# A decode step of two attention and two gated layers on one core: TensorE multiplies a constant in its pauses

## The chip, the cores and the metric

The kernel runs on one core of one Trainium2 chip. What counts is the device time of one execution in microseconds. A core has a matrix engine (TensorE, PE in the profile, with PEld for its weight loads), a vector engine (VectorE, DVE), an engine for activation functions and copies (ScalarE, ACT), a general engine (GpSimd, POOL) and SyncE (SP), which here does nothing but issue the loads from HBM. Sixteen DMA engines move what is issued. SBUF is the memory on the core that matmuls read, PSUM (eight banks of 128 x 512 numbers in f32) the one they write.

## The reference

Four sequences decode one token each. The same attention layer and the same gated layer are applied twice:

```
x = A_x                                    # 4 x 1 x 512
x = x + attention(layernorm(x))            # 32 q heads, 8 kv heads, head size 128
x = x + gated(layernorm(x))
x = x + attention(layernorm(x))            # same weights, same caches
x = x + gated(layernorm(x))

attention(x): q = x @ wq                   # 512 x 4096
              k, v = last 2048 rows of the caches (4 x 8 x 8192 x 128)
              softmax(q k^T / sqrt(128)) v, then @ wo      # 4096 x 512
gated(x):     (sigmoid(x @ w_gate) * (x @ w_up)) @ w_down  # 512 x 1792, 1792 x 512
```

All of it is bf16 in memory. The K and V that are read are 16.8 MB each; 69.4 MB are read from HBM in all, since most of V, wq and the gated layer's weights are read once per layer.

## The kernel before, in words

**Plan, order and semaphores.** The program first makes a list of operations (`P.op`): engine, name, an estimated duration, what it reads and writes by token, and which PSUM banks it touches. `_schedule` orders each engine's list by estimated start times; only TensorE's operations that are written after the first gated layer (`P.chain = True`) keep the order in which they are written. The loads on SyncE always keep theirs. `_assign_sync` then gives every operation one semaphore that its last instruction raises, and the waits that its readers need. Two operations of TensorE need no wait between them. An operation that touches a bank waits for another engine's operations on that bank.

**Memory.** SBUF has 50 slots of 128 x 2048 bf16. The 16 K tiles (1 MB, one for each kv head and pair of sequences) take 32 slots and stay for both attentions. V tiles, wo, wq and the gated weights go through what is left. A load into a place that was used before waits until its last reader has raised its semaphore. In the first gated layer the places form a ring: gate loads go where V lay, up loads go where gate, wq or V lay, down loads go where gate and up lay, the second wq's loads where up and down lay.

**The first attention** (`attn_first`) goes over the kv heads 0 to 7. For head h: VectorE transposes the K tiles in place (line 927, four pieces of 128 x 1024); TensorE writes a mask into a bank (line 945) and adds the scores (line 956, 16 matmuls of 512 columns, four column strips of the array side by side); VectorE takes the maximum (line 969 and after); ScalarE takes the exponential (line 984); TensorE turns the probabilities with the constant matrix `perm` (line 997); ScalarE copies them (line 999) and VectorE transposes them (line 1004). Then TensorE multiplies by V (line 1047: 32 matmuls of 8 columns for each of a head's two V tiles), scales and permutes (lines 1056, 1066, 1071) and multiplies by wo into the bank WB (line 1238). Head h + 2 is begun before head h is ended.

**The first gated layer** (`glu`) begins with the layer norm: a sum (line 794), a matmul with 1/512 (line 799), differences, a second matmul for the variance (line 820). Gate and up take four loads each; every load brings four matmuls of 448 columns on four column strips (line 1426), written to bank WB. VectorE transposes each result (line 1435). w_down comes in four loads with 12 or 16 matmuls of 4 columns each (line 1496), added in bank CB; line 1513 adds the sum to x.

**The second q and the second attention.** A layer norm again, then 32 matmuls with wq (line 868) as eight parts, of which the last loads arrive during the layer. The second attention (`attn_second`) goes over the heads 7 to 0 with K as it lies in SBUF: mask and scores on the same lines, V with 512-column matmuls (line 1130), VectorE's transposes behind them (line 1140). The second gated layer ends with w_down on line 1471 and the store.

The diff touches `layer_norm`, `softmax_unit`, `pv_unit`, `wo_unit` and `glu`.

## Time and profile before

| | |
|---|---|
| runs | 176.71, 176.71, 177.76 us (median 176.71) |
| profiled execution | 177.47 us, span 175.8 us |
| TensorE busy | 107.3 us, 1663 matmuls |
| VectorE busy | 105.6 us |
| ScalarE, GpSimd busy | 34.0, 23.3 us |
| loads | 69.38 MB, 96.5% of sixteen engines' span |
| mean granted clock, as recorded | 0.947 |
| chain that ended last | DMA 38%, VectorE 31%, TensorE 23% |

The page cuts the span into 40 slices of 4.4 us and gives the busy share of each in tenths; PEclk is the recorded clock of TensorE in tenths of full speed. The other views answer from the same execution: the timeline of one engine (start and duration in us, engine, line, what is written and read, how many), sums over windows (for each engine busy time and number of instructions, then clock, share of the DMA engines, GB/s), the chain that ended last (start, duration, what), and the list of loads with the time from issue to landing. A matmul's duration there holds its own latency, so sixteen in a row take less than sixteen times their mean. Landing times of single loads, their sixteen parts (one for each DMA engine) and the clock's records are read from the same trace.

### The profile page before, as it was taken

The page shows a single profiled execution, that of the slowest core. Times are in us where ns is not written, and L with a number is a line of the kernel's source. Part 1 is how long each engine was busy: PE and PEld are TensorE (multiplying, and loading weights), DVE is VectorE, ACT ScalarE, POOL GpSimd, SP SyncE. Part 2 cuts the span into 40 slices and gives each one's busy share as a digit, 9 for nine tenths or more (in the row PEclk, how much of TensorE's full clock was granted, in tenths as well). Part 3 has the DMA queues.
Part 4 walks back from the last instruction along what each step waited for, and adds up shares of the span by engine and source line. Part 5 has one row for each costly group of instructions (what it writes and reads, how often), then busy time and mean ns, then how long its engine had stood idle before and what let it go on. Part 6 is the DMA issues. An engine that isn't in the chain of part 4 may idle for free.

```text
span 175.8 us, 3937 instructions
## 1 busy us (share of the span) xinstructions
PE 107.3 (61%) x1663; PEld 55.3 (31%) x1663; DVE 105.6 (60%) x260; ACT 34.0 (19%) x89; POOL 23.3 (13%) x94
## 2 busy tenths in 40 slices
PE   0536246268566272661765566558975999877692
PEld 0203112023334151340444452143321344345531
DVE  6307997994957748377323831316496699944343
ACT  2002021322303003020030010102132354541011
POOL 6100010101101001010010000002011334534000
PEclk9999999999999999999999999999996599997558
DMA  5999999999999999999999999999999999999970
GB/s 187 423 429 429 420 421 423 406 423 423 427 412 411 422 421 420 425 406 426 423 406 425 406 399 405 403 401 390 403 394 408 425 425 416 420 420 418 419 282 5
DMA packets 12370, 69.64 MB, mean 396 GB/s; under 512 B 1336, under 2 KB 1472, under 8 KB 6336
## 3 DMA queue, kind: packets, MB, share of 16 engines
q1 hardware_dynamic: 12344, 69.38, 96.5%
q8 instruction: 13, 0.21, 0.5%
q14 instruction: 5, 0.04, 0.1%
q10 hardware_dynamic: 8, 0.00, 0.0%
HBM read 69.37 MB, written 0.00 MB: 395 GB/s over the span
## 4 chain that ended last, share of the span: by engine, by line
DMA 38%; DVE 31%; PE 23%; issue 3%; ACT 2%; SPq 1%; POOL 1%; POOLq 0%; DVEq 0%
DMA arena<-in_A_v_cache_dram 20%; DVE arena L927 10%; PE ps L956 8%; DMA arena<-in_A_wq_dram 6%; DMA arena<-in_B_w_gate_dram 5%; DVE small L969 4%; DMA side<-in_A_wq_dram 4%; DMA arena<-in_B_w_up_dram 3%; PE ps L945 3%; PE ps L1130 2%; DVE arena L1140 2%; DVE small L973 2%; DVE side L1004 2%; PE ps L1047 2%; PE ps L1426 2%
## 5 line engine op out<-in xcount | busy, mean ns | idle before, releaser
L927 DVE STREAM_TRANSPOSE arena<-arena 128x1024 f32<-128x1024 f32 x32 | 37.0, 1204 | 0.1
L1047 PE MATMUL ps<-side,arena 128*128 128x8 bf16 x576 | 18.1, 168 | 13.2 <-DMA arena<-in_A_v_cache_dram 13.1
L956 PE MATMUL ps<-arena,side 128*32 128x512 bf16 x256 | 25.8, 539 | 0.1
L1047 PEld LDWEIGHTS ps<-side,arena 128*128 128x128 bf16 x576 | 16.7, 104 | 19.6 <-DMA arena<-in_A_v_cache_dram 17.7
L969 DVE TENSOR_REDUCE small<-ps 128x1 f32<-128x512 f32 x16 | 10.9, 678 | 17.5 <-PE ps L956 17.4
L984 ACT ACTIVATE side<-ps,small 128x512 bf16<-128x512 f32 x16 | 11.0, 687 | 35.4 <-PE ps L1066 18.3
L945 PE MATMUL ps<-small,msk_s 128*32 128x512 bf16 x64 | 8.6, 530 | 14.7 <-DVE arena L927 14.1
L920 ACT CAST side<-ps 128x256 bf16<-128x256 f32 x16 | 5.9, 371 | 34.2 <-PE ps L956 25.9
L999 ACT CAST side<-ps 128x512 bf16<-128x512 f32 x16 | 9.4, 585 | 14.0 <-PE ps L997 14.0
L1013 POOL CAST small<-small 128x1 bf16<-128x1 f32 x9 | 1.7, 187 | 76.1 <-ACT side L984 76.1
L956 PEld LDWEIGHTS ps<-arena,side 128*32 128x32 bf16 x256 | 8.3, 121 | 10.7 <-issue 7.9
L997 PE MATMUL ps<-side,perm 128*128 128x512 bf16 x16 | 8.1, 507 | 4.7 <-ACT side L984 4.7
L1130 PE MATMUL ps<-arena,side 128*32 128x512 bf16 x112 | 8.5, 431 | 1.4 <-ACT side L984 1.4
L868 PE MATMUL ps<-arena,xn 128*4 128x512 bf16 x60 | 7.3, 577 | 3.2 <-DMA arena<-in_A_wq_dram 2.9
L1426 PE MATMUL ps<-arena,xn 128*4 128x448 bf16 x60 | 6.9, 537 | 3.2 <-DMA arena<-in_B_w_up_dram 1.5
L1056 DVE TENSOR_TENSOR onb<-ps,rinv 128x16 bf16<-128x16 f32 x9 | 1.7, 185 | 10.9 <-PE ps L1047 10.8
L1004 DVE STREAM_TRANSPOSE side<-side 128x256 f32<-128x256 f32 x16 | 6.9, 433 | 2.0 <-ACT side L999 1.8
L915 PE MATMUL ps<-side,eyew 32*128 32x64 bf16 x64 | 5.7, 220 | 3.3 <-ACT side L920 2.4
L945 PEld LDWEIGHTS ps<-small,msk_s 128*32 128x32 bf16 x64 | 1.7, 98 | 17.9 <-DVE arena L927 16.2
L1435 DVE STREAM_TRANSPOSE side<-ps 128x448 f32<-128x448 f32 x4 | 2.5, 634 | 7.3 <-PE ps L1426 7.3
L1140 DVE STREAM_TRANSPOSE arena<-ps 128x512 f32<-128x512 f32 x7 | 4.9, 700 | 2.6 <-PE ps L1130 2.6
L915 PEld LDWEIGHTS ps<-side,eyew 32*128 32x128 bf16 x64 | 3.4, 108 | 8.8 <-ACT side L920 5.4
(133 smaller groups left out, 136.5 us busy)
## 6 DMA issues: line engine op xcount, KB each, us to landing
arena<-in_A_v_cache_dram SPq DMA_DIRECT2D x26, 1024.0 KB, 14.8
arena<-in_A_k_cache_dram SPq DMA_DIRECT2D x16, 1024.0 KB, 24.9
arena<-in_A_wq_dram SPq DMA_DIRECT2D x4, 1024.0 KB, 7.9
arena<-in_A_wo_dram SPq DMA_DIRECT2D x3, 1024.0 KB, 26.7
arena<-in_A_v_cache_dram SPq DMA_DIRECT2D x5, 512.0 KB, 7.0
arena<-in_A_wq_dram SPq DMA_DIRECT2D x5, 512.0 KB, 7.0
arena<-in_B_w_up_dram SPq DMA_DIRECT2D x4, 448.0 KB, 6.0
arena<-in_B_w_gate_dram SPq DMA_DIRECT2D x2, 896.0 KB, 17.0
```

Source lines behind the costliest of these rows:

```text
L915: last = pe.matmul(dst[:, :, a * REP:(a + 1) * REP], eyew[32 * hh:32 * hh + 32, 96 - 32 * a:224 - 32 * a], src, start=True, stop=True)
L927: P.op("vector", "T%d_%d" % (h, t), c_dve(1024), lambda v, v32=v32: v.transpose(v32, v32), r=[("slot", 4 * h + t)], w=[("slot", 4 * h + t)])
L945: last = pe.matmul(ps[32 * gi:32 * gi + 32, bank, :], msk_s[:, :], msk_m[:, :].unsqueeze(1).broadcast_to([128, 256, 2]), start=True, stop= ...
L956: last = pe.matmul(ps[32 * gi:32 * gi + 32, bank, :], qbd[:, q0:q0 + 32], kt[:, cp // 2, cp % 2, jh * NJ:(jh + 1) * NJ, :], start=False, s ...
L969: lambda v: v.tensor_reduce(nmax[:, k2:k2 + 1], ps[:, bank, :], AXX, ALU.max),
L984: lambda a: a.activation(prow[:, :].rearrange("p (m x t) -> p m x t", x=32, t=2), ps[:, bank, :].rearrange("p (m t x) -> p m x t", x=32, t ...
L999: P.op("scalar", "pc" + tag, c_act(512), lambda a: a.copy(prow[:, :], ps[:, pb, :]), r=[("ppb", pb)], w=[("prow",)], banks=(pb,))
L1004: P.op("vector", "pt" + tag, c_dve(256), lambda v: v.transpose(et, prow[:, :].bitcast(F32)), r=[("prow",)], w=[("e", k2)])
L1047: last = pe.matmul(ps[:, ob, bp * 8:bp * 8 + 8], slot_ap(ss[j // NJ])[:, j % NJ * 128:(j % NJ + 1) * 128], ev[:, j % 2, j % 16 // 2, x0:x0 ...
L1130: last = pe.matmul(ps[32 * g:32 * g + 32, ob, :], ew[:, g, mq, t], src.rearrange("p (m t d) -> p t m d", t=2, d=128)[:, t], start=(n == 0) ...
L1140: P.op("vector", "tv" + tag, c_dve(512), lambda v: v.transpose(tv, ps[:, ob, :]), r=[("pso", k2, 0), ("pso", k2, 1)], w=[("tv", k2)], bank ...
L1426: last = pe.matmul(ps[32 * g:32 * g + NB, gub[n], 0:NF], xn[:, c * NB:(c + 1) * NB], src[:, g * NF:(g + 1) * NF], start=(c == 0), stop=(c ...
```

## The change

A new function `keep_warm` issues n matmuls with `perm` as weights and `perm` (repeated where more than 128 columns are asked for) as the moving operand, into PSUM columns that nobody reads, or reads only after a matmul that starts anew. `keep_op` makes an operation of them that follows the TensorE operation written last. They are put:

- ahead of and behind the scores of kv head 7 in the first attention (12 and 4 of 448 columns);
- behind seven of the V tiles, from the second of head 4 on (4 each, 3 behind the last), and between the two halves of the last wo (3);
- around the first gated layer's first norm (12 of 32 columns, 2 of 512), behind five of its eight gate and up parts (11 of 64), behind gate and behind up (16 of 32 each), ahead of w_down (2 of 512), behind each of its parts (2, 2, 2, 1 of 512), and behind the second q's first norm matmul (1 of 512).

Inside an operation the constants stand behind the matmul that raises the semaphore.

```diff
+        def keep_warm(pe, n, bank, c0, w):
+            last = None
+            for _ in range(n):
+                dst = ps[:, bank, c0:c0 + w]
+                src = perm[:, 0:min(w, 128)]
+                if w > 128:
+                    dst = dst.rearrange("p (a x) -> p a x", x=64)
+                    src = perm[:, 0:64].unsqueeze(1).broadcast_to([128, w // 64, 64])
+                last = pe.matmul(dst, perm[:, :], src, start=False, stop=False, skip_group_check=True)
+            return last
+
+        def keep_op(name, n, bank, c0, w, after=()):
+            return P.op("tensor", name, n * (w / 2.4 + 10.0), lambda pe: keep_warm(pe, n, bank, c0, w),
+                        w=[("cb",)] if bank == CB else [], banks=(bank,),
+                        after=tuple([o for o in P.ops if o.eng == "tensor"][-1:]) + tuple(after))
+
+        WFREE = REP * NX
+        WARM_V = {"0.%d_1" % (HKV - 4): 4, "0.%d_0" % (HKV - 3): 4, "0.%d_1" % (HKV - 3): 4, "0.%d_0" % (HKV - 2): 4,
+                  "0.%d_1" % (HKV - 2): 4, "0.%d_0" % (HKV - 1): 4, "0.%d_1" % (HKV - 1): 3}
...
+            if tag == "G0":
+                keep_op("kwL", 12, CB, SAVED_P, 32)
             P.op("tensor", "ln_sum" + tag, tm["pe_f32"],
...
+            if tag == "G0":
+                keep_op("kwG", 2, WB, 0, 512)
+            if tag == "Q":
+                keep_op("kwQ", 1, WB, 0, 512)
...
+            if tag == "0.%d" % (HKV - 1):
+                keep_op("kwS", 12, WB, WFREE, 512 - WFREE, named("pp0.%d" % (HKV - 2)))
             P.op("tensor", "S" + tag, (16 if wait else 20) * tm["pe_row"], e_s,
...
+            if tag == "0.%d" % (HKV - 1):
+                keep_op("kwT", 4, WB, WFREE, 512 - WFREE)
...
+                    keep_warm(pe, WARM_V.get("%s_%d" % (tag, bp), 0), WB, WFREE, 512 - WFREE)
                     return last
                 P.op("tensor", "PV%s_%d_%d" % (tag, h, bp), 2 * NJ * tm["pe_pair"], e_pv,
-                     r=[("slot", x) for x in ss] + [("e", k2)], w=[("pso", k2, bp)], banks=(ob,))
+                     r=[("slot", x) for x in ss] + [("e", k2)], w=[("pso", k2, bp)],
+                     banks=(ob, WB) if "%s_%d" % (tag, bp) in WARM_V else (ob,))
...
+                    if half < REP and r0 == 0:
+                        keep_warm(pe, 3, WB, WFREE, 512 - WFREE)
...
+                        if k == 0 and (c or n) and c < NC - 1:
+                            keep_warm(pe, 11, WB, NF, 512 - NF)
...
+                if k == 0:
+                    keep_op("kw%d" % n, 16, CB, SAVED_P, 32)
...
+            keep_op("kw2", 2, WB, 0, 512)
...
+                    keep_warm(pe, 2 if b < NFC else 1, WB, 0, 512)
                     return last
```

More of the change, by code (lines that the diff above doesn't have):

```diff
@@ L1499, in e_d @@
                                              start=(fc == 0 and c == 0), stop=(fc == NFC - 1), skip_group_check=True)
+                    keep_warm(pe, 2 if b < NFC else 1, WB, 0, 512)
                     return last
                 P.op("tensor", "gd%d_%d" % (k, a), (b - a) * NC * tm["pe_pair"], e_d,
-                     r=stok(s, (b - a) * D) + [("hT",)] + hts, w=[("cb",)], banks=(CB,))
+                     r=stok(s, (b - a) * D) + [("hT",)] + hts, w=[("cb",)], banks=(CB, WB))
                 done(name)
```

## The prediction

> **What bounds the kernel now.** I read the times first. The profiled execution took 177.47 us, 1.7 us more than its span of 175.8, and lies inside the runs shown (176.71 to 177.76, median 176.71). One per cent, 1.8 us, is about what a measurement of this kernel can tell from no change. My sum is made against 177.47, and its result is then set beside the median.

> The page's slices come next.

> ```profile
> PEclk9999999999999999999999999999996599997558
> DMA  5999999999999999999999999999999999999970
> ```

> The DMA engines are full from the second slice to the 38th, so 69 MB of loads are a stream without a hole. PEclk seems to say that TensorE had its full clock until slice 30. The timeline of TensorE denies it: the same scores (line 956, 16 matmuls of 512 columns) at two times.

> ```profile
> 83.05 1.93 PE L956 MATMUL ps<-arena,side 128*32 128x512 bf16 x16
> ...
> 144.61 1.08 PE L956 MATMUL ps<-arena,side 128*32 128x512 bf16 x16
> ```

> At 83 us TensorE ran at half speed; the first clock record of the trace begins at 126.41, and before it the row shows a default. TensorE is slow from the start to 126.4. The chain that ended last says where this matters.

> ```profile
> 115.67 6.58 DMA side<-in_A_wq_dram
> 122.29 0.60 PE ps L868 x4
> ...
> 124.20 1.86 PE ps L956 x14
> ...
> 133.97 1.90 PE ps L1130 x16
> ...
> 172.39 0.98 PE ps L1471 x56
> ```

> Up to 122.25 the chain is mostly loads: TensorE's work there is beside the stream. From 122.29 it holds compute alone, on a slow TensorE until 126.4 and again from 133.23 to 140.06. But the stream is only just ahead of it, as the issue list and the windows at the end show.

> ```profile
> arena<-in_B_w_down_dram SPq DMA_DIRECT2D x1, 256.0 KB, 21.9
> ...
> 169.00:170.00 1.00, 1.00 (x14) 0.62 (x14) 0.65 (x1) 0.21 (x2) 0.00 (x0) 0.50 0.81 318
> 170.00:171.00 1.00, 1.00 (x20) 0.44 (x16) 0.45 (x3) 0.52 (x3) 0.00 (x0) 0.61 0.26 100
> ```

> The last load, the end of w_down, was issued at 149.83 and landed 21.9 us later, at 171.71. TensorE starts w_down at 172.39, **0.68 us after the last landing**. (Last columns of the windows: granted clock, DMA share, GB/s.)

> **What moves the clock.** The records change only on a grid of 3.41 us: slow to fast at 126.41, back at 133.23, fast at 140.06, slow at 160.54, fast at 170.78. So I looked at windows cut on that grid.

> ```profile
> 129.82:133.23 3.41, 1.83 (x26) 0.81 (x26) 3.14 (x11) 0.47 (x3) 0.94 (x4) 1.00 1.02 399
> 153.71:157.13 3.42, 2.57 (x31) 1.79 (x31) 2.24 (x7) 1.38 (x4) 0.94 (x4) 1.00 1.00 413
> 157.13:160.54 3.41, 2.80 (x65) 1.78 (x66) 1.58 (x5) 1.42 (x4) 1.67 (x7) 1.00 1.02 422
> ```

> The third is busier than the second (2.80 against 2.57 us) and yet the clock falls after it. It is full of 8-column matmuls, so I count streamed columns, not busy time. 16 matmuls of 512 columns on four column strips take 0.89 us fast (line 1130 at 154.24), so 512 columns are 0.22 us fast, 0.43 slow. In column time at the fast rate, as a share of a window: 0.35 and 0.36 (first and third) dropped the clock, 0.40 (second) and 0.47 kept it; from slow, 0.37 and 0.38 did not raise it, 0.44 and 0.46 did. **The line lies near 0.39 of a window, either way.** The start of the grid I take as free in each execution.

> [...]

> **The change, part by part.** It adds 157 matmuls of a constant (46 of 448 columns, 44 of 32, 55 of 64, 12 of 512) with a weight load each; nothing is removed, and the order on VectorE, ScalarE, GpSimd and the DMA queue stays. They total 31,680 columns, 13.7 us fast or 27 us slow by the 512-column price, all between 78.7 and 120 us, where TensorE has pauses. Semaphores are still raised by the last real matmul, so only what is next on TensorE waits.

> 1. *Last K tiles.* TensorE idles from 78.73 to 82.65, for the transposes. 12 constants (448 columns: 0.38 us slow, 0.19 fast) fill 78.7 to 82.6-83.2; with the scores and 4 more behind, TensorE is dense for 6 to 8 us, so a whole grid window is full and the clock rises between 81.4 and 84.8. The scores may start 0.5 us late and run 1 us shorter. Cover: the V tile after next lands at 86.80. Cost nothing.

> 2. *V tiles.* One lands every 2.49 us (1 MB); 4 constants stand behind each of six, 3 behind the last. Two tiles need 8 x 448 constant columns and about 1,400 of real work, 2.1 us of 4.97: 0.42 on average, but a 3.41 us window that catches only one group holds 0.75 + 0.45 = 1.2 us, 0.35. So it will often fall. When slow, two tiles take 8 x 0.38 + 2 x 0.87 (line 1047) + about 1.2 for the rest = 6.0 us against 4.97: TensorE lags by 1 us per pair, some 2.5 us at the last V tile, and then holds only 0.31 to 0.33, so it does not recover there. The constants between the halves of the output weights and ahead of the mean add up to 2.3 us slow, 1.1 us fast, partly in pauses: first gate matmul up to 0.3 us late if fast, 3.5 us if slow.

> Who waits: the loads of w_up, w_down and wq go to places that these matmuls free. w_up's third load was issued at 106.72 and the load ahead of it landed at 111.28, a lead of 4.6 us; 1.1 us are left at 3.5 us late. At the start of the kernel the first packet moved 1.04 us after its issue. So the stream just holds, and this costs between 0 and 1 us (fewer than nothing is excluded: no load is issued earlier where the engines are full). I take 0.

> 3. *Gate, up, down.* Gate and up: 11 x 64 constants and the four real matmuls are 0.48 us per 1.12 us of load, 0.43; the clock comes back there. Slow they fill 0.45 + 0.59 = 1.04 of 1.12 us, so a lag stays but does not grow. Down: two of 512 per 1.25 us, 0.36 alone, about 0.42 from 113.5 to 119.7 with the constants around it. All of it is covered by the wq load that lands at 122.25 (the sixteen q matmuls ahead of it end at 121.6 today), unless rival C holds.

> 4. *From 122.29.* If the clock is fast: line 868 twice 0.60 to 0.39, line 945 0.62 to 0.40, line 915 0.39 to 0.28, line 956 1.90 to 1.08: **1.5 us** earlier at 126.1. Behind it VectorE carries the chain to 133; then TensorE waits for the softmax, as before, and the window there (0.35) may drop again; if it does not, 133.97 to 140.7 loses another 2.6 us (line 1130 0.86 and 0.4, 997 0.2, 945 0.2, 956 0.84, small ones 0.2). From 140 to 152 VectorE is full and nothing is gained.

> 5. *More instructions.* The 13 fetches of 16 KB on the instruction queue belong to TensorE's 3,326 instructions, so 314 more are 1.2 fetches. One at 30.44 made one of the sixteen parts of a load land 1.06 us late from there on. Cost 0 to 1.1 us, if it hits the slowest engine; taken as 0.

> **The sum.** The compute chain gains 1.5 to 4.1 us, but only 0.68 until w_down's last load is late next. After the landing at 171.71 its 8 matmuls need 0.3 us: the last matmul ends at 172.0 in place of 173.37. 177.47 - 1.4 = **176.1 us**, 0.3% under the median: no change that can be told.

> **Rivals.**
> - *B, it doesn't do what it says.* The window before 122.3 holds kwQ (0.22), sixteen q matmuls (0.87) and little else, 1.1 to 1.2 us, 0.33 to 0.35: if a grid edge falls just before 122.3, the second attention starts slow as now. Going through where the edge can lie, this is about one case in three, and in some of them part 4's second half makes up for it. Time as before, 176.7 to 177.6: 177.0.
> - *C, slower.* The constants themselves become the queue ahead of the second q. If the clock is slow from the last up load (landed 113.49) on, 4.7 us of constants, 5.3 us of real work and 1.5 us of waits stand ahead of the matmuls that need the last of the first wq loads: 125.0. Some 1.3 us of the constants lie inside those waits, which leaves 123.7, 1.4 us behind 122.29; the second attention then starts late and as slow as now: 177.47 + 1.4 = 178.9, more if part 2's lag is still there. It decides where the window that ends near 113.5 is under 0.39. Against it: the gate stage's own 0.43.
> - *D, faster.* The last landing is not fixed. The sixteen engines end between 169.2 and 171.3; the windows after 169 hold 0.81 + 0.26 + 0.03 = 1.1 us of full work, so evenly shared they would end at 170.1, 1.2 us sooner. If fetches fall otherwise, and compute gains over 2 us, 176.1 - 1.2 = 174.9, or a little less.

> **How the numbers follow.** Forecast 0.48 (175.3 to 176.7), B 0.20, C 0.17, D 0.15. D is taken as faster by over 1% (under 174.94), C as slower (over 178.48), the others as the same: 0.15, 0.68, 0.17. The range 174.8 to 177.9 leaves out C and little of D.

> **What would show it.** Right: line 956 near 1.08 us at its first use in the second attention; the first q matmul there still released by the wq load; the w_down matmuls of the end waiting for a load; line 1047's tiles after 92 us starting late behind slow constants. Wrong: the last landing well before 171, or w_down still waiting for VectorE; a DMA share below 0.9 between 105 and 122 us (the stream starved); or a first q matmul that starts long after its load.

## The result, and the profile after

The changed kernel takes **177.76 us** (median of 22 runs, 176.09 to 179.71); the kernel before, run beside it, 176.62 (22 runs, 176.04 to 177.76). The ratio is 1.0058 with a 95% interval of 1.0037 to 1.0080: slower by 0.6%, where I had forecast 0.3% faster, that is, nothing. (The ratio leaves out three runs of the changed kernel, 178.74 to 179.71 us, that fell into a slower state.) I had taken one per cent as the least that can be told from no change; with 22 runs of each kernel, 0.6% can. The profiled execution took 178.39 us, span 176.6.

The page of the kernel after, TensorE's recorded clock, the DMA engines and what they moved, in 40 slices:

```profile
PEclk9999999999999999999978978997597899995555
DMA  5999999999999999999999999999999999999970
GB/s 185 427 427 423 427 423 421 406 419 425 421 419 415 415 419 429 419 404 429 412 415 424 403 403 388 393 412 395 412 319 395 423 423 423 416 418 423 417 305 4
```

The clock moves a good deal earlier than before: its records show full speed from 83.67 to 90.49, 93.91 to 104.15, 107.56 to 121.21 and 128.04 to 134.87 us. (Ahead of 83.67 there is no record and the row shows nines again, though twelve constants of 448 columns take 4.68 us there, 0.39 each.) But it falls at 121.21, just ahead of the second attention, and the stream has a thin slice (319 GB/s, at 128 to 132 us).

TensorE's timeline at that place (start, duration, line, tiles, number; in brackets the idle time before and what ended it):

```profile
120.72 0.39 PE L894 MATMUL ps<-arena,xn 128*4 128x512 bf16 x4 [0.71 <-DMA arena<-in_A_wq_dram]
121.82 0.60 PE L894 MATMUL ps<-arena,xn 128*4 128x512 bf16 x4 [0.71 <-DMA arena<-in_A_wq_dram]
...
123.11 0.60 PE L894 MATMUL ps<-side,xn 128*4 128x512 bf16 x4 [0.16 <-DMA side<-in_A_wq_dram]
...
124.95 1.90 PE L982 MATMUL ps<-arena,side 128*32 128x512 bf16 x16
```

The constants are not in the way here: TensorE stands idle for 0.71 us twice, **waiting for loads of wq**. The load that opened the second attention at 122.29 before opens it at 123.11, and the first scores take 1.90 us, as slow as before.

The chain that ended last, from there on:

```profile
115.45 7.61 DMA side<-in_A_wq_dram
123.11 0.60 PE ps L894 x4
...
125.01 1.86 PE ps L982 x9
...
134.77 1.85 PE ps L1163 x16
...
144.06 0.61 DVE arena L1173
...
154.16 0.89 PE ps L1163 x16
...
162.93 0.87 PE ps L1078 x32
...
172.55 1.69 PE ps L1510 x56
```

The wq load was issued 0.22 us earlier than before (115.45 against 115.67) and yet ended 0.8 us later: 7.61 us in place of 6.58. Against the profile of before the chain seems to make this up by 154 us and to lose 0.7 us in the last line alone (1.69 against 0.98 us, a matter of the clock). That comparison misleads: executions of the kernel before differ among themselves by up to 1.7 us. A second profile of it, of a faster execution (176.78 us), happens to have the clock of after from 128 us on (fast from 128.14 to 134.96, slow to 138.38, fast again). Its chain, at the same steps:

```profile
122.15 0.53 PE ps L868 x4
...
124.00 1.86 PE ps L956 x12
...
133.77 1.05 PE ps L1130 x16
...
142.69 0.64 DVE arena L1140
...
152.80 0.89 PE ps L1130 x16
...
161.37 0.87 PE ps L1047 x32
...
170.98 1.69 PE ps L1471 x56
```

Step by step the kernel after is behind by 0.96, 1.01, 1.00, 1.37, 1.36, 1.56 and 1.57 us, and its execution by 1.61. **The loss begins at the one wq load**: 0.96 of the 1.57 us are there, and go down a chain of compute to the end. The 0.37 us added near 134 us are the clock: at 134.77 the kernel after starts 16 matmuls just as its fast stretch ends (134.87) and needs 1.85 us; the other starts them 1.00 us earlier and needs 1.05. Another 0.20 us come between 154 and 163 us; what adds them is not shown.

Why is that load late? A load comes in sixteen parts and counts as landed with the last (before, the last part comes at 122.25 us and the matmul that waits for it starts at 122.29). From the trace, when the parts of this load came (us; the ninth and the last four of sixteen), and the fetches of TensorE's instructions near it:

```
               9th part      last four parts                   fetches of 16 KB started at
before            121.46     121.68  121.73  121.76  122.25    103.00  119.03
before, 2nd       121.58     121.74  121.75  121.78  121.84    103.14  118.42
after             121.40     121.56  121.57  121.63  123.06    100.25  108.96  118.50
```

Fifteen parts of after are in by 121.63, earlier than before; one is at 123.06. It is late from the load on that was in flight when the fetch of 118.50 ran: the load ahead by two has fifteen parts by 119.12 and one at 120.68, the load before that none behind. The DMA view of both kernels, cut to the first 122 us, counts the fetches (queue, packets, MB, share of sixteen engines); before, then after:

```profile
q8 instruction: 8, 0.13, 0.4%
```

```profile
q8 instruction: 9, 0.15, 0.5%
```

### The profile page after: what moved, and what is told of

It is laid out like the page before. It is cut to its first block, busy times and chain, and to the rows that moved or that the text cites. A ratio compares the mean times of both kernels' runs of the same rounds, so it can differ in the third digit from the quotient of the medians.

```text
span 176.6 us, 4239 instructions
## 1 busy us (share of the span) xinstructions
PE 116.9 (66%) x1808; PEld 62.4 (35%) x1820; DVE 105.7 (60%) x260; ACT 34.1 (19%) x89; POOL 23.3 (13%) x94
## 2 busy tenths in 40 slices
DMA  5999999999999999999999999999999999999970
## 4 chain that ended last, share of the span: by engine, by line
DMA 55%; PE 18%; DVE 15%; SPq 6%; issue 2%; ACT 1%; POOL 1%; POOLq 0%; DVEq 0%
DMA arena<-in_A_v_cache_dram 48%; SPq L401 6%; DMA side<-in_A_wq_dram 4%; PE ps L1078 3%; DMA arena<-in_B_w_up_dram 3%; PE ps L791 2%; DVE small L1000 2%; PE ps L1163 2%; DVE arena L1173 2%; PE ps L982 2%; PE ps L1461 2%; DVE arena L1178 1%; DVE arena L596 1%; DVE side L1035 1%; PE ps L1271 1%
## 5 line engine op out<-in xcount | busy, mean ns | idle before, releaser
L982 PE MATMUL ps<-arena,side 128*32 128x512 bf16 x256 | 24.8, 520 | 0.0
L791 PE MATMUL ps<-perm 128*128 128x64 bf16 (+3 forms) x157 | 22.4, 283 | 0.5 <-issue 0.3
L791 PEld LDWEIGHTS ps<-perm 128*128 128x128 bf16 x157 | 8.9, 105 | 7.1 <-issue 5.6
L1163 PE MATMUL ps<-arena,side 128*32 128x512 bf16 x112 | 8.3, 422 | 1.4 <-ACT side L1015 1.4
L1461 PE MATMUL ps<-arena,xn 128*4 128x448 bf16 x60 | 5.8, 474 | 1.3 <-DMA arena<-in_B_w_up_dram 0.7
```

Of the source, the lines that this page charges most:

```text
L791: last = pe.matmul(dst, perm[:, :], src, start=False, stop=False, skip_group_check=True)
L982: last = pe.matmul(ps[32 * gi:32 * gi + 32, bank, :], qbd[:, q0:q0 + 32], kt[:, cp // 2, cp % 2, jh * NJ:(jh + 1) * NJ, :], start=False, s ...
L1163: last = pe.matmul(ps[32 * g:32 * g + 32, ob, :], ew[:, g, mq, t], src.rearrange("p (m t d) -> p t m d", t=2, d=128)[:, t], start=(n == 0) ...
L1461: last = pe.matmul(ps[32 * g:32 * g + NB, gub[n], 0:NF], xn[:, c * NB:(c + 1) * NB], src[:, g * NF:(g + 1) * NF], start=(c == 0), stop=(c ...
```

## The experiments

All ratios are to the kernel before, run on the same chip beside it (medians 176.59 to 176.72). The last columns are of the one profiled execution; between the two of the kernel before, the landing of the wq load differs by 0.41 us. Where a row shows 8 fetches, the ninth starts after that load has landed.

| | ratio, 95% interval | fetches ahead of 122 us | 9th starts | last wq part (before: 122.25, 121.84) |
|---|---|---|---|---|
| after | 1.0058 (1.0037 to 1.0080) | 9 | 118.5 | 123.06 |
| e1_tiny | 1.0087 (1.0054 to 1.0121) | 9 | 118.7 | 123.11 |
| e2_first | 1.0004 (0.9977 to 1.0031) | 8 | 126.8 | 122.61 |
| e3_second | 1.0055 (1.0025 to 1.0084) | 9 | 119.3 | 122.92 |
| e4_second_r | 1.0019 (0.9990 to 1.0047) | 9 | 119.4 | 122.98 |
| e5_shift128 | 1.0063 (1.0038 to 1.0089) | 9 | 118.6 | 123.18 |
| e6_shift64 | 1.0007 (0.9989 to 1.0024) | 8 | 125.9 | 121.98 |
| e7_after64 | 1.0090 (1.0057 to 1.0123) | 10 | 112.5 | 123.44 |
| e8_down_r | 1.0165 (1.0131 to 1.0198) | 8 | 125.8 | 121.79 |
| e9_few_r | 0.9999 (0.9966 to 1.0033) | 8 | 122.9 | 122.28 |
| e10_few | 1.0016 (0.9981 to 1.0051) | 8 | 123.2 | 122.43 |
| e11_shift256 | 1.0095 (1.0059 to 1.0131) | 10 | 103.3 | 123.62 |

### e1_tiny: the same instructions with almost no column time

```diff
         def keep_warm(pe, n, bank, c0, w):
             last = None
             for _ in range(n):
+                w = 8
                 dst = ps[:, bank, c0:c0 + w]
```

> All 157 constants stay where they are, but each streams 8 columns in place of 32 to 512: the same instructions, almost no time on TensorE (157 x 0.03 us, 4.4 us spread over 40) and no help for the clock. Three theories for the 1.1 us by which the changed kernel is slower. LATE: slow constants hold TensorE, loads that wait for its semaphores are issued late, the DMA engines run dry; then this kernel is like the kernel before, within 0.3 us. FETCH: the 314 instructions are fetched by the same DMA engines and make the slowest of them slower; then it is slower by 0.5 to 1.1 us, like the changed one. CLOCK: what counts is only how the second attention starts; it starts slow here as before, 0 us.

Ratio 1.0087. The loads of w_up are issued on time (106.69 against 106.72), the clock is slow until 127.86 (126.41 and 128.14 in the kernel before), and the wq load still ends at 123.11. So what the constants take of TensorE's time is not needed for the loss, and their number is enough; LATE falls.

### e2_first and e3_second: half of the constants each

```diff
 # e2_first: these and w_down's are left out
-                keep_op("kwL", 12, CB, SAVED_P, 32)
-                keep_op("kwG", 2, WB, 0, 512)
-                keep_op("kwQ", 1, WB, 0, 512)
-                            keep_warm(pe, 11, WB, NF, 512 - NF)
-                    keep_op("kw%d" % n, 16, CB, SAVED_P, 32)
```

```diff
 # e3_second
-        WARM_V = {"0.%d_1" % (HKV - 4): 4, ...
+        WARM_V = {}
-                keep_op("kwS", 12, WB, WFREE, 512 - WFREE, named("pp0.%d" % (HKV - 2)))
-                keep_op("kwT", 4, WB, WFREE, 512 - WFREE)
-                        keep_warm(pe, 3, WB, WFREE, 512 - WFREE)
```

> Only the constants up to the last wo: 12 + 4 around the scores of head 7, 27 behind V tiles, 3 between the halves of wo. Nothing in the gated layer, so the clock is slow again by 122 us. LATE: the first gate matmul is late by the 3 constants of wo and what TensorE still lags, 0.2 to 0.8 us in the profile, and the time rises by 0.2 to 0.6 us. FETCH: 92 instructions, a third of a fetch: 0 to 0.4 us. CLOCK: 0 us, the second attention starts as before.

> Only the constants from the gated layer's first norm on (111 of 157); the clock is slow when they begin. LATE: 12 of 32 and 2 of 512 columns ahead of the first gate matmul cost up to 0.9 us there, gate and up then keep pace: 0.4 to 1.0 us slower. FETCH: 222 instructions, 0.9 of a fetch: 0.3 to 0.8 us. CLOCK: where the window before 122 us is full enough, the first scores of the second attention take 1.1 us in place of 1.9 and the time falls by up to 1 us; where it is not, 0 us.

The 46 wide constants up to the last V tiles and wo cost nothing that can be told (1.0004). The 111 from the first norm on cost all of it (1.0055). With them the ninth fetch starts at 119.26 and the wq load ends at 122.92; without them it starts at 126.8.

The one trace of e2 does not look like its median. The execution took 177.66 us, one of the longer of twelve (176.09 to 178.12, median 176.64), and in it the first scores of the second attention start at 124.66, as in e3. There the *eighth* fetch, at 109.26, is followed by one part of w_up's third load that lands 0.88 us behind the other fifteen; the loads of w_down end 0.7 to 0.8 us later than in the kernel before, and the second q starts at 120.48 in place of 119.72. So a fetch that is not the ninth can do it too; how often it does in the executions that were not traced, no run shows.

### e4_second_r: e3, and the clock held up to the second attention

```diff
+                if k == 1 and i == 1 and c in (1, 2):
+                    keep_op("kwR%d" % c, 20, CB, SAVED_P, 32)
```

(behind the second and third part of the second q)

> As the run with the gated layer's constants alone, and 20 more of 32 columns behind the second and the third part of the second q, where TensorE waits 0.7 us each for the next wq load. They lift the window before 122 us from 0.32 of its column time by 0.08 to 0.16, over the line at 0.39. CLOCK: the first scores of the second attention take 1.1 us in the profile, the V loads that wait for them are issued 1 us or more earlier, and the time is 0.5 to 1.5 us under that of the run without these 40. LATE and FETCH: no gain from them, 0 to 0.3 us more than that run.

The clock stays up from 108.5 to 156.3. TensorE's timeline of e4 at the start of the second attention:

```profile
123.03 0.39 PE L893 MATMUL ps<-side,xn 128*4 128x512 bf16 x4 [0.59 <-DMA side<-in_A_wq_dram]
...
124.56 1.09 PE L983 MATMUL ps<-arena,side 128*32 128x512 bf16 x16
```

It starts as late as in after (the fetch is there, at 119.4), but the scores end at 125.65 in place of 126.03 before. The ratio comes back to 1.0019: much of what e3 loses seems to be won back by the fast clock (the intervals of the two overlap).

### e5_shift128 and e6_shift64: the kernel before with early instructions, and nothing else

```diff
+        def shift(n):
+            def e(pe):
+                last = None
+                for _ in range(n):
+                    last = pe.matmul(ps[:, WB, 0:8], perm[:, :], perm[:, 0:8], start=False, stop=False, skip_group_check=True)
+                return last
+            P.op("tensor", "shift", n * 50.0, e, r=perms, w=[], banks=(WB,),
+                 after=tuple([o for o in P.ops if o.eng == "tensor"][-1:]))
...
+            if tag in ("0.1", "0.2", "0.3", "0.4"):
+                shift([32, 32, 32, 32][int(tag[2]) - 1])     # e6: 16 each
```

> The kernel before with 128 multiplications of 8 columns (read by nobody) behind four early score steps of the first attention, between about 20 and 60 us, where TensorE waits for K tiles anyway. They are 256 instructions, so every fetch of TensorE's instructions moves forward by about one: in the kernel before, the 7th and 8th of the profiled fetches start at 103.0 and 119.0 us and the 9th at 132.2; here the 9th should start near 117 us, as the 9th did in the kernel after (118.5) and in the version with 8 columns everywhere (118.7). Nothing is added between 80 us and the end. FETCH (which DMA engine a 16 KB fetch delays goes by the number of the fetch, and the 9th hits the one that is last): the last load of the second q lands at 122.9 to 123.1 instead of 122.25, the second attention starts 0.7 to 0.9 us later, 177.3 to 178.3 us, ratio 1.004 to 1.009. PLACE (the loss comes from instructions that stand between 105 and 122 us, by some way other than the fetches): landing at 122.25, 176.4 to 176.9, ratio 0.998 to 1.002.

> As the one before, with 64 such multiplications in place of 128. By the order of the instructions the 8th fetch should start near 112 us and the 9th near 125, so none lies at 117 to 120 us. FETCH: if the fetch of 112 us meets a DMA engine that is ahead of the others, the last load of the second q lands at 121.8 to 122.3 and the time is 176.0 to 176.8 (ratio 0.996 to 1.001); if it meets the one that is last, the landing is at about 122.9 and the ratio 1.003 to 1.007, and the trace must show that one part alone is late by about 1 us from 112 us on. PLACE: as before, 176.4 to 176.9, landing at 122.25.

This is the test on which the cause rests. In e5 nothing of the change is there, and nothing is added behind 60 us. (The columns written are, other than the expectation says, columns of the output projection's sums, so the output differs; e11's expectation says it for all of these.) The chain of e5, and the same step of e6:

```profile
115.60 7.58 DMA side<-in_A_wq_dram
123.22 0.60 PE ps L877 x4
...
122.28 0.53 PE ps L877 x3
```

In e5 the load is issued 0.07 us earlier than before and lands 0.93 later, ratio 1.0063: as the change itself. With half as many (e6) the eighth fetch starts at 107.0 (expected: near 112) and the ninth at 125.9, the load ends at 121.98 and the ratio is 1.0007. The two intervals do not overlap. (In the traced execution of e6 the clock is up from 123.41, in that of e5 from 128.37, so their later steps are not compared.) Instructions that stand near 105 to 122 us (PLACE) are not needed for the loss.

The parts of the loads in e5 show why it is the *ninth* fetch. Sixteen parts in order, us from their median, of a load behind the 1st, 4th, 8th and 9th fetch:

```
1st   -0.2 -0.1 -0.1 -0.1 -0.1 -0.1 -0.0 -0.0  0.0  0.0  0.1  0.1  0.1  0.1  0.2  1.5
4th   -0.2 -0.2 -0.2 -0.2 -0.1 -0.1 -0.0 -0.0  0.0  0.1  0.1  0.8  1.4  1.4  1.4  1.5
8th   -1.3 -1.3 -1.2 -1.1 -1.0 -0.9 -0.6 -0.2  0.2  0.3  0.3  0.3  0.4  0.4  0.4  0.5
9th   -1.3 -1.3 -1.2 -1.1 -1.0 -0.9 -0.6 -0.2  0.2  0.3  0.4  0.4  0.4  0.4  0.5  1.9
```

With the first eight fetches the number of late parts grows, one fetch, one more part by 0.8 to 1.5 us, until about half of them are late together. The end of a load is set with the first of them and hardly moves with the next seven. The ninth meets a part that is late already, and the end of every load behind it moves by 1.4 us at once. In after, e1, e3, e4, e5, e7 and e11, where the ninth comes ahead of the last wq load, the last part falls back by 0.8 to 1.3 us against the mean of the sixteen with it; with the second to eighth it does so by 0.3 us at the most; in e6 the ninth does the same (1.2 us) behind that load. The count is not the whole of it: in e2, e9 and e10 the eighth fetch (109.26, 114.25 and 114.44) already moves the end of the loads, by 0.9, 0.5 and 0.75 us, and the ninth adds 0.4 to 1.0. Why, no run shows. That a part is one DMA engine's share fits the packets of before: between 8 and 28 us each of the sixteen parts of a load of 1 MB is eight packets of 8 KB and one of 4 bytes, and just ahead of the first twelve fetches 16.2 to 16.6 of the loads' packets are in flight on the average, during them 14.9 to 15.6. But the trace does not name engines, and no run shows whether the ninth fetch goes to the engine of the first.

### e7_after64: the change, with its fetches moved

> The kernel after, with the 64 early multiplications of 8 columns. Its fetches should start near 104, 115 and 119 us instead of 100, 109 and 118.5. FETCH: one fetch more falls between the start of w_up's loads and the second q's last landing; which engines the two meet decides, so the landing of that load is 122.2 if neither meets the last one (then 176.4 to 177.0, ratio 0.998 to 1.002), 123.1 if one does (177.4 to 178.2, ratio 1.004 to 1.009), and the time goes with the landing either way. PLACE: as the kernel after, 177.4 to 178.2, wherever the fetches fall and whenever that load lands.

Ratio 1.0090, above that of after (the intervals overlap). The ninth fetch, at 112.54, meets the last load of w_up: fifteen parts by 113.55, the last at 114.89, 1.4 us behind the load's end in the kernel before. TensorE waits for it (1.66 us), the window of the clock there holds 0.23 of column time, the clock falls, and w_down's constants run at half speed (1.03 us for two of 512; 0.59 to 0.60 in after). So the wq loads are issued late as well (115.67 before, 117.42 here), and the second q starts at 122.67 in place of 119.72. FETCH foretold a late landing (123.1; it was 123.44) but not this: once the clock is lost, the constants are the queue, and the matmuls that need that load start at 125.00, 1.6 us behind its landing. PLACE's 177.4 to 178.2 does not fit either. (This is read from one execution, of 179.41 us; the twelve spread from 176.66 to 181.28.)

### e8_down_r: only w_down's constants, and those behind the second q

```diff
+            keep_op("kw2", 2, WB, 0, 512)
+                    keep_warm(pe, 2 if b < NFC else 1, WB, 0, 512)
+                keep_op("kwQ", 1, WB, 0, 512)
+                    keep_op("kwR%d" % c, 20, CB, SAVED_P, 32)
```

> The kernel before with a constant of 512 columns at the second q's norm, 20 of 32 columns behind each of the second and third part of the second q, and the change's constants from w_down's tiles on; nothing of the change ahead of 117 us. The instructions ahead of 119 us are those of the kernel before but for a few, so its 8th fetch should stay at 118 to 119.5 us and the last load of the second q should land at 122.2 to 122.4. FETCH with CLOCK: the landing is on time and the window of the clock that ends near 122 us holds about 0.48 of column time instead of 0.33, so the second attention starts at 122.3 with its scores at about 1.1 us instead of 1.9: 175.2 to 176.2 us, ratio 0.991 to 0.997, the fastest of all. PLACE: the 40 small ones behind the second q stand in the place that costs, so 176.5 to 177.3, ratio 0.999 to 1.004.

I expected the fastest and got the slowest, 1.0165. The load was on time (121.79), as FETCH said, but the clock was not. Four rows of TensorE's timeline in e8, and below them the start of the second q in the kernel before:

```profile
114.86 1.03 PE L791 MATMUL ps<-perm 128*128 128x512 bf16 x2 [0.76 <-DVE side L1460]
...
117.58 1.01 PE L791 MATMUL ps<-perm 128*128 128x512 bf16 x2
...
121.48 1.02 PE L889 MATMUL ps<-arena,xn 128*4 128x512 bf16 x8
122.44 0.71 PE L791 MATMUL ps<-perm 128*128 128x32 bf16 x20
...
119.72 1.88 PE L868 MATMUL ps<-arena,xn 128*4 128x512 bf16 x16 [0.26 <-DVE xn L802]
```

Without the constants at gate and up the clock is still slow when w_down begins. Two constants of 512 columns take 1.0 us in place of 0.6, all of it in the queue ahead of the second q, which starts at 121.48 in place of 119.72. The forty small ones between its parts add to the queue (0.71 and 0.69 us), and the matmuls that open the second attention start at 124.86 in place of 122.29. The clock rises at 123.97, when it is too late. This is rival C of the prediction.

### e9_few_r and e10_few: the same column time in fewer instructions

```diff
 # against e4_second_r (e10: kwR left out)
-                keep_op("kwL", 12, CB, SAVED_P, 32)
-                keep_op("kwG", 2, WB, 0, 512)
+                keep_op("kwG", 3, WB, 0, 512)
-                    keep_op("kwR%d" % c, 20, CB, SAVED_P, 32)
+                    keep_op("kwR%d" % c, 9, CB, SAVED_P, 32)
-                if k == 0:
-                    keep_op("kw%d" % n, 16, CB, SAVED_P, 32)
+                if k == 0 and n:
+                    keep_op("kw%d" % n, 4, CB, SAVED_P, 32)
-            keep_op("kw2", 2, WB, 0, 512)
+            keep_op("kw2", 3, WB, 0, 512)
```

NINTH is the theory that the loss comes with the ninth fetch, where it starts ahead of the landing of the last wq load.

> As e4_second_r, with 60 constants fewer ahead of 122 us at nearly the same column time: none at the first norm's sum but one of 512 columns more behind it, none behind the gate, 4 in place of 16 behind up, one of 512 more ahead of w_down's first tile, 9 in place of 20 behind the second and third part of the second q. [...] NINTH: 60 constants are 120 instructions, and in e4 107 start between its ninth fetch (119.37 us) and 122.6, so here the ninth starts at 122.3 us or later; the second q's last load lands at 121.7 to 122.4 instead of 122.98, and as the clock is fast there, as in e4, the second attention gains: 175.0 to 176.0 us, ratio 0.990 to 0.997, faster than both kernels. If the number of the fetch does not matter, as e4: 176.4 to 177.1, ratio 0.999 to 1.004. If the column time left is too little for the clock, w_down's constants run at half clock and hold the second q up, as in e8: 178 and more.

> As e9_few_r without the constants behind the second q's parts, so it is e3_second (the change's constants from the gated layer's first norm on; ratio 1.0055, its ninth fetch at 119.26 us) with 38 constants fewer at nearly the same column time. NINTH: the ninth fetch starts 76 instructions later, at 123 to 125 us; the second q's last load lands at 121.8 to 122.4 us instead of 122.92, and the loss of e3 is gone: 176.3 to 176.9 us, ratio 0.998 to 1.002. If e3's loss is the constants' own time or their place, it stays: 177.2 to 178, ratio 1.003 to 1.008, whenever that load lands.

The ninth fetch went where it was meant to, behind the wq load: 122.93 and 123.16. The load ends at 122.28 and 122.43, and what e3 lost is gone in e10 (1.0016; the intervals of the two overlap, so the landing times carry more of the proof than the ratios). But e9, with the ninth fetch behind that load and a fast clock (its second head's scores begin 1.1 us before those of the kernel before), is no faster: 0.9999. The end of its chain tells why:

```profile
150.30 21.74 DMA arena<-in_B_w_down_dram
172.04 0.04 issue
172.08 0.41 PE ps L1502 x6
```

Compute now waits for the last load, which lands at 172.04, no earlier than in the kernel before (171.71 and 171.72). Faster compute has nothing to gain behind it.

### e11_shift256: two fetches more, none near

```diff
-                shift([32, 32, 32, 32][int(tag[2]) - 1])
+                shift([64, 64, 64, 64][int(tag[2]) - 1])
```

> As e5_shift128, with 256 early multiplications of 8 columns in place of 128 (they are added to columns of the output projection's sums, so the output differs; this holds for e5, e6 and e7 too). They are 512 instructions, so two fetches more lie ahead of 122 us than in the kernel before: its 7th and 8th (103.0 and 119.0 us) become the 9th and 10th. NINTH (the fetches go round eight DMA engines, the ninth meets one that is late already, the tenth and those behind it only bring the others up to it): the second q's last load lands late once, at 122.8 to 123.3 us as in e5, and the ratio is 1.003 to 1.009. If every further fetch costs alike: the landing is at 123.8 to 124.3 and the ratio 1.010 to 1.016. If the stream's pause at 104 to 108 us lets the engine of the ninth catch up: the landing is at 122.0 to 122.4 and the ratio 0.999 to 1.003.

Neither sum fits exactly: the load ends at 123.62 and the ratio is 1.0095, both between NINTH and the theory that every fetch costs alike. The parts decide for NINTH, as far as its one late step goes; which engines the fetches meet, no trace shows. The ninth fetch starts at 103.25; from the wo load in flight there on, the last part is 1.4 to 1.7 us late. The gate loads are 1.5 us late with it, the up loads that wait for their places are issued 1.5 us late (108.22 for 106.72), and so every load behind lands about 1.4 us later, to the end (173.20). The tenth fetch, at 120.2, only brings another part up to the last (123.50 and 123.62). One step of 1.4 us in all; it passes whole where the loads behind hang on it, and 0.8 to 0.9 us of it where the wq load alone does.

### e12_before: the kernel before once more

> The kernel before, unchanged, for a second profile of it. Its executions fall into two groups, 176.0 to 176.8 and 177.1 to 177.9 us; the profiled one (177.47) is of the second, its store issued at 174.07, behind a last w_down that began at 172.39 when the last load (171.71) had long landed. Two bounds at the end: A, the last landing plus about 1.1 us (e4: 171.60 to 172.76; e10: 172.00 to 173.05), and B, the compute chain, whose length goes with where the clock's windows fall. If that is right, a profile of the first group ends on A: last landing at 171.5 to 172.0, the last 4 to 8 multiplications of w_down behind it, the store issued 1.0 to 1.2 us after it; and one of the second group ends on B as the first profile did. Rival: the two groups differ in when the last load lands (by about 1 us), with the same end behind it.

176.78 us, the second profile used above. The last landing is 171.72, as in the first (171.71), so the rival falls: the spread of the kernel before lies in its chain of compute (last w_down at 170.98 against 172.39), and that goes with the clock (fast to 134.96 here, to 133.23 there). Bound A is not reached here: the last w_down starts ahead of the landing and is slow, and the store is issued 1.65 us behind the landing, not 1.0 to 1.2.

## Why the prediction was wrong, step by step

- **What bounds the kernel: right, with a hole.** The chain of compute from the wq load on, and the last landing just behind it, are what the runs found (e9 ends on the second). But I took 122.25, the start of that chain, as given by a full stream. The stream stayed full; it is *one of sixteen parts* that sets the start, and that part moved.
- **Part 5, the step that failed: "Cost 0 to 1.1 us, if it hits the slowest engine; taken as 0".** The count was right (14 fetches for 13) and so was the delay of one part. Its value is the upper end: I had looked at the first fetch alone and not at what eight of them add up to. By the ninth about half of the parts are late, and it hits one of these, in the seven kernels named at e5. It costs 0.81 to 0.96 us at the wq load and 1.57 at the end of the one pair of profiles with the same clock; 1.1 us in the medians. e5 shows it alone.
- **Part 4 failed as rival B foresaw.** The window 117.80 to 121.21 held 0.32 of column time and the clock fell at its end; the second attention was slow: the 1.4 us that the sum takes off were not there. B's price, "as before, 177.0", lacked the fetch. Where the clock did hold (e4, e9), its first steps were 1.1 to 1.2 us shorter, a little less than my 1.5.
- **The cap held.** I allowed no more than 1.4 us for the fast clock since the last landing comes next. In e9 that took all of it.
- **Parts 1 to 3 were right in what they cost.** The scores of the last K tile began 0.47 us late and the clock rose at 83.67 (forecast: 81.4 to 84.8). V tiles left no lag (line 1099 at 103.25 against 103.19), because the clock fell there once only, at 90.49; it fell again at 104.15, and three constants of 448 then took 1.27 us. The first gate matmul was 1.16 us late (forecast 0.3 to 3.5), the up loads were issued 0.8 to 1.1 us late, and the last part of these loads was not late at all (112.26 against 112.38): the parts that run ahead of the others took it. The V tiles' and wo's constants cost nothing in e2's median.
- **Rival C** does not occur in after, since the clock is up from 107.56 to 121.21. e7 and e8 show that it is real and what it costs where the clock is down: 1.6 us (e7, fetch included) and 2.9 us (e8). **Rival D**, an earlier last landing, occurs in no profile (171.60 at the least).

The sum was 176.1; with the fetch's 1.0 to 1.6 us and no gain at 122 us it is 178.5 to 179.1 by its own measure, the profiled 177.47, which was a slower execution of the kernel before; by the median of before, 176.62, the fetch makes 177.6 to 178.2, and 177.76 was measured.

## What to carry to other kernels

Instructions that do nothing still have to be fetched (in e5 the ninth fetch starts at 118.6 us in place of 132.2). Where a load stream is full and something waits for the end of a load, count TensorE's instructions ahead of that load: 128 matmuls more moved it by 0.9 us here (e5), and nearly the same column time in fewer, wider matmuls by less (landing at 122.43 us in e10 against 122.92 in e3). A filler that is to keep the clock up should begin where the clock is up already or its time is free; ahead of a step on the critical path, at half speed, it was just a queue (e8: 1.03 us for two constants of 512 columns, the second q 1.76 us late). And before speeding up a chain, look at what it would wait for next: here the last load, at once (172.04 us in e9).

## What the runs showed of the hardware

```profile
104.15:107.56 3.41, 3.41 (x35) 1.65 (x36) 1.51 (x8) 0.06 (x1) 0.00 (x0) 0.50 1.03 408
117.80:121.21 3.41, 2.42 (x29) 0.90 (x28) 2.07 (x8) 0.62 (x1) 0.38 (x2) 1.00 1.04 398
```

TensorE was busy for 2.42 us of the window after which it lost its clock.
